# Put-off work spread over 32 groups instead of 8, and sum and difference in one VectorE operation

## The chip, the cores and the metric

The kernel runs on one core of a Trainium2 chip. The metric is the device time of one execution in microseconds. Before the change three executions took 2817.58, 2814.88 and 2814.3 us, a median of 2814.88 us.

The engines are named as in the profile: PE is TensorE's matmul, PEld its weight load, DVE is VectorE, ACT is ScalarE, POOL is GpSimd, SP is SyncE, which here only issues DMAs.

## What is computed

A Fourier transform along two axes, a gated two-matrix network with two matrices behind it, and a greedy routing of 24576 tokens to 8 experts of 3072 places each:

```python
def _attn_ref(x):                       # x: 8 x 3072 x 256
    X = np.fft.fft(x, axis=1)
    X = np.fft.fft(X, axis=2)
    return X.real.astype(np.float32)

def _moe_ref(x, w1, w2, w3, w_out):     # 256 -> 1024 -> 1024 -> 256
    a = x @ w1
    b = x @ w2
    h = a * b @ w3
    return (h @ w_out).astype(np.float32)

def _moe2_ref(x, w_gate, w1, w2):
    logits = x @ w_gate
    order = np.argsort(-logits.flatten())
    # greedy: best (token, expert) pairs first, each expert takes N // E tokens
    ...
    for e in range(E):
        mask = assigned == e
        h = np.maximum(x[mask] @ w1[e], 0.0)
        out[mask] = h @ w2[e]
```

## The kernel before

**Two stages.** Stage A makes the rows (transform, first network) and their logits, stage B routes them and runs the experts. All products run in split form: a value is a high part and a low part of type fp32r, and `mm3` makes three matmuls of one product (high by high, high by low, low by high).

**Stage A** works in 384 steps: 8 batches `b`, 2 sets `st`, 3 blocks `q`, 8 slices `f` of the hidden width. The 8 steps of one (b, st, q) are a group; there are 48 groups, and a group makes 512 rows. In one step, `front` makes the odd part `us` (6 matmuls of 256 columns) and the even part `ue` (one of 512 columns, six of 256) in two PSUM tiles `l1` of four. ACT copies `us` to `qs` (four buffers), DVE makes `ue + qs` and `ue - qs` into `pm` (one buffer) and multiplies its two halves into `ab`, which is `qs` again. One step later `parts` splits `ab`: ACT writes the high part `ah`, POOL the low part `al` (three buffers each). Three steps later `back` multiplies `ah` and `al` by the combined matrix `W` (`l2`: 12 matmuls of 264 columns, 256 of the row and 8 of the logits) into four PSUM tiles `acc`, one for each 128 of the 512 rows. At the group's end ACT moves them out and `store` writes rows (`xs_d`) and logits (`L`).

**Put off.** The last 8 groups (`ASIDE`) do not run `l2`. Their `ah` and `al` go to DRAM (`away`, two DMAs of 256 KB in a step on SP's queue), those of the very last group (`KEPT`) straight into the places of the two transform tables. Only their logits are made: `logits` runs two matmuls of 512 columns with the gate columns of `W` as weights (16 and 8 columns of weights), and at a group's end ACT copies the 16 x 512 result, PE turns it in four small products into an `acc` tile, and DVE writes it to `L`. In stage B `putoff` runs the 768 missing matmuls of 256 columns (L1371) while the first routing works.

**Beside the steps.** `dft_set` makes the next set's transform in four parts spread over the steps of `DFT_AT`. `fold_batch` makes the next batch's inputs, nearly all on POOL: 1.3 units of work are handed out in a step (`FOLD`), which spreads one batch's folding over some 26 steps, from the end of a batch's first group to the start of its fifth. `middle` (L921) is a small product for eight single rows in the last set.

**What sets the order.** PE, DVE, ACT and POOL run in the order in which the code is written (`manual_schedule`); the DMAs on SP are placed by the scheduler. In every step the order is `front`, `back` of three steps before, the multiplication, `parts` of the step before, then the things put off by `later`.

In stage A no matmul of type fp32r moves fewer than 256 columns; the second table is read 256 wide although a part of it has 192 or 193 columns:

```python
        w = 193 if kind % 2 else 192
        return tabs["B"][p0:p1, hl, base + t * w: base + t * w + 256]
```

Of the kernel before, what the change touches and what calls it, by code (L numbers as in the profile page):

```python
# [9 lines left out]
F32 = mybir.dt.float32  # L10
# [12 lines left out]
NT = N // 128  # L23
# [2 lines left out]
NF = FF // 128  # L26
FMAX = 3.4028234663852886e38
XW = 260
ASIDE, KEPT = 8, 1
SHARE = 864  # L30


# [192 lines left out]
@with_exitstack  # L225
def body(ctx, tc, I, out, nb=NB, dbg=None):
    nc = tc.nc
    vec, act, pool = nc.vector, nc.scalar, nc.gpsimd
    dram = ctx.enter_context(tc.tile_pool(name="dram", bufs=1, space=bass.MemoryType.DRAM))
    xs_d = dram.tile([N, XW], F32, name="xs_d")  # L230
    ed = dram.tile([2, NB, 3, 768], F32R, name="ed")
    em = dram.tile([3, NB], F32R, name="em")
    sp_d = dram.tile([8, NB, 128], F32R, name="sp_d")
    md = dram.tile([NB, D], F32, name="md")
    away = dram.tile([max(ASIDE - KEPT, 1), NF, 128, 2, 512], F32R, name="away")
# [24 lines left out]
    stage_b(tc, I, out, k)  # L260
# [19 lines left out]
def stage_a(ctx, tc, I, nb, k):  # L280
# [532 lines left out]
    def front(g):  # L813
# [10 lines left out]
                extras(steps[i])  # L824
        e3 = e3t[0]
        n = number(g)
        spill = 0 <= n < k.aside - KEPT

        qs = work.tile([128, 512], F32, name="qs", bufs=4)
        ab = qs.rearrange("p (s c) -> p s c", s=2)  # L830

        us, ue = l1(), l1()
        for w in range(2):
# [15 lines left out]
        if n >= 0:  # L849
            k.putoff[n, f] = None if spill else (ah, al)  # L850

        def parts():
            act.activation(ah, qs, AF.Copy)  # L853
            (vec if n == k.aside - 1 and f in LAST else pool).tensor_tensor(al, qs, ah, op=ALU.subtract)  # L854
# [18 lines left out]
        at = f % 4 * 1024  # L873
        return places[key][:, at:at + 512], places[key][:, at + 512:at + 1024]

    def logits(n, f, ahl, j0):

        if f == 0:
            acct[0] = accs(n % 4)
        a = acct[0]  # L880
# [4 lines left out]
        lt = work.tile([2 * E, 512], F32, name="xo")  # L885
        u = accs((n + 2) % 4)[:, :4 * E].rearrange("p (i e) -> p i e", i=4)
# [5 lines left out]
        later(1, lambda: act.activation(lt, a[:2 * E], AF.Copy))  # L892
        later(2, turn)
        later(3, lambda: vec.tensor_copy(L[:, :, j0:j0 + 4].rearrange("p e j -> p j e"), u))

    def back(g, ahl):
        b, st, q, f = g
        n = number(g)
        if n >= 0:
            logits(n, f, ahl, (b * 6 + st * 3 + q) * 4)  # L900
            return
        if f == 0:
            acct[0] = [accs(i) for i in range(4)]
        acc = acct[0]
        l2(acc, ahl[0], ahl[1], f, 4)
        if f < NF - 1:
            return
        j0 = (b * 6 + st * 3 + q) * 4
        for h in range(2):
            xo = work.tile([128, 2, 264], F32, name="xo")  # L910
            act.activation(xo[:, 0], acc[2 * h][:, :264], AF.Copy)
            (vec.tensor_copy(xo[:, 1], acc[2 * h + 1][:, :264]) if EV else act.activation(xo[:, 1], acc[2 * h + 1][:, :264], AF.Copy))
            later(1, lambda xo=xo, j=j0 + 2 * h: store(xo, j))

    def store(xo, j):
        pool.tensor_copy(L[:, :, j:j + 2].rearrange("p e j -> p j e"), xo[:, :, D:])
        pool.tensor_copy(xo[:, :, D:D + 4], sc["tok"][:, j:j + 2, None].to_broadcast([128, 2, 4]))
        nc.sync.dma_start(k.xs_d[j * 128:(j + 2) * 128].rearrange("(i p) d -> p i d", p=128), xo[:, :, :XW])


    def middle():  # L921
# [22 lines left out]
        xo = work.tile([128, 264], F32, name="qs", bufs=4)  # L944
        act.activation(xo[:NB], acc[:NB, :264], AF.Copy)
        nc.sync.dma_start(k.md, xo[:NB, :D])
        for b in range(nb):
            p, j = DUP[b]
            if b == nb - 1:
                yield  # L950
            nc.sync.dma_start(L[p:p + 1, :, j], xo[b:b + 1, D:])
            if j // 4 < nb * 6 - k.aside:
                nc.sync.dma_start(k.xs_d[j * 128 + p:j * 128 + p + 1, :D], xo[b:b + 1, :D])
        yield

# [62 lines left out]
def stage_b(ctx, tc, I, out, k):  # L1018
# [315 lines left out]
    def putoff():  # L1334
# [311 lines left out]
```

## Time and profile before

| what | us |
|---|---|
| median of three executions | 2814.88 |
| the profiled execution | 2810.5 |
| its span, first to last instruction | 2808.7 |
| stage A, steps of the first 40 groups | 111.0 to 1202.5 |
| steps of the last 8 groups (put off) | 1202.5 to 1384.5 |
| end of stage A, until the logits are complete | 1384.5 to 1394.7 |
| put-off products in stage B | 1394.7 to 1496.4 |
| rest of the first routing | 1496.4 to 1540 |
| experts | 1540 to 2808.7 |

The profiled execution took 4.4 us less than the median of the others. Busy shares over the whole span are PE 95%, PEld 87%, DVE 76%, ACT 47%, POOL 54%; a share is an average over stages with different limits. A matmul's recorded time is longer than its distance to the next one, because they overlap; what PE can do is read from the distances between starts.

### The profile page before, as it was taken

What the parts mean: (1) busy time and instruction counts of PE and PEld (TensorE: products, weight loads), DVE (VectorE), ACT (ScalarE), POOL (GpSimd) and SP (SyncE); (2) the same over time, 40 slices, a digit from 0 to 9 for tenths busy, and PEclk for the clock granted to TensorE, in tenths of its full rate; (3) what the DMA queues carried; (4) which work ended last, traced back from release to release, by engine and by line L of the source; (5) the groups of instructions that cost most, each with busy time, mean ns of one, the idle gap of its engine ahead of it and who ended that gap; (6) DMA issues with size and microseconds to landing.
All of it is one profiled execution on the core that took longest, in us unless ns stands there. A gap on an engine that the chain in (4) does not pass through costs nothing.

```text
span 2808.7 us, 51817 instructions
## 1 busy us (share of the span) xinstructions
PE 2674.4 (95%) x19903; PEld 2454.0 (87%) x19903; DVE 2135.4 (76%) x3795; ACT 1323.0 (47%) x2383; POOL 1518.0 (54%) x1529
## 2 busy tenths in 40 slices
PE   4999999999999999999996999989999999999998
PEld 2899999999999999987796788878888888889997
DVE  8788787978878797888877888788787878862222
ACT  2344444444444444444363747466573746543332
POOL 7295775939577593964304244353535435363532
PEclk8999999999999999999997999999999999999999
DMA  6410110101011011145394112211212122121211
GB/s 232 133 54 32 39 46 24 54 32 54 32 39 47 24 52 34 52 162 200 128 338 154 36 65 54 69 50 46 76 43 73 48 67 54 43 68 43 76 46 35
DMA packets 104705, 207.32 MB, mean 74 GB/s; under 512 B 35178, under 2 KB 60442, under 8 KB 99338
## 3 DMA queue, kind: packets, MB, share of 16 engines
q1 hardware_dynamic: 81000, 131.02, 13.7%
q0 software_dynamic: 22224, 72.58, 8.0%
q8 instruction: 157, 2.57, 0.4%
q14 instruction: 90, 0.74, 0.1%
q10 hardware_dynamic: 1234, 0.41, 0.1%
HBM read 118.15 MB, written 80.28 MB: 71 GB/s over the span
## 4 chain that ended last, share of the span: by engine, by line
PE 73%; DVE 17%; ACT 3%; issue 2%; DMA 1%; POOL 1%; another core or an unknown queue 0%; DVEq 0%; ACTq 0%; POOLq 0%; SPq 0%
PE yp L1483 13%; PE l L220 7%; PE l L222 7%; PE l L221 7%; PE acc L804 5%; PE acc L800 5%; PE acc L801 5%; PE hp L220 4%; PE hp L221 4%; PE hp L222 4%; DVE oR L1086 4%; PE l L836 3%; DVE W L1466 2%; ACT ja L1081 2%; PE hp L1371 2%
## 5 line engine op out<-in xcount | busy, mean ns | idle before, releaser
L854 POOL TENSOR_TENSOR al<-qs,ah 128x512 fp32r<-128x512 f32 x376 | 513.4, 1365 | 406.2 <-ACT ah L853 311.4
L1483 PE MATMUL yp<-FA,W 128*128 128x256 f32 x3040 | 622.0, 286 | 17.8 <-DVE W L1466 8.4
L1483 PEld LDWEIGHTS yp<-FA,W 128*128 128x128 f32 x3040 | 497.8, 190 | 44.6 <-ACT yo L1489 14.9
L859 DVE TENSOR_TENSOR qs<-pm 128x512 f32<-128x512 f32 x384 | 427.4, 1113 | 41.2 <-DVE pm L843 1.8
L853 ACT ACTIVATE ah<-qs 128x512 fp32r<-128x512 f32 x376 | 237.2, 631 | 358.2 <-DVE qs L859 317.7
L1466 DVE SCALAR_TENSOR_TENSOR W<-hp,W 128x512 fp32r<-128x512 f32 x336 | 230.1, 687 | 227.0 <-ACT W L1462 205.0
L1483 PE MATMUL yp<-FB,W 128*128 128x256 f32 x1520 | 388.0, 282 | 0.0
L842 DVE TENSOR_TENSOR pm<-l,qs 128x512 f32<-128x512 f32 x384 | 264.7, 689 | 149.4 <-PE l L222 116.2
L840 ACT ACTIVATE qs<-l 128x512 f32<-128x512 f32 x384 | 227.0, 591 | 235.3 <-PE l L222 220.0
L220 PE MATMUL hp<-tabA,tabB 128*128 128x512 f32 x768 | 319.5, 416 | 0.9 <-ACT tabA L1432 0.9
L1493 POOL DMA_INDIRECT out_dram<-yo,oi x188 | 191.7, 1020 | 231.3 <-DMA out_dram<-yo,oi 217.8
L1462 ACT ACTIVATE W<-hp 128x512 fp32r<-128x512 f32 x336 | 197.2, 593 | 251.6 <-PE hp L222 232.7
L221 PE MATMUL hp<-tabA,tabB 128*128 128x512 f32 x768 | 304.0, 396 | 6.0 <-DVE tabA L1436 6.0
L1483 PEld LDWEIGHTS yp<-FB,W 128*128 128x128 f32 x1520 | 287.9, 189 | 14.3
L800 PE MATMUL acc<-W,ah 128*128 128x264 f32 x1120 | 283.6, 284 | 0.0
L801 PE MATMUL acc<-W,ah 128*128 128x264 f32 x1120 | 283.3, 284 | 0.0
L1086 DVE TENSOR_SCALAR_CACHE_REDUCE oR<-oR,nx 128x1536 uint16<-128x1536 uint16 x196 | 281.4, 1459 | 0.0
L843 DVE TENSOR_TENSOR pm<-l,qs 128x512 f32<-128x512 f32 x384 | 261.2, 680 | 0.0
L1407 POOL DMA_INDIRECT xt<-xs_d,idx x192 | 194.9, 1015 | 109.1 <-issue 49.9
L1457 POOL TENSOR_TENSOR W<-xo,W 128x512 fp32r<-128x512 f32 x48 | 66.6, 1387 | 336.8 <-ACT W L1455 321.1
L222 PE MATMUL hp<-tabA,tabB 128*128 128x512 f32 x624 | 246.7, 395 | 0.0
L220 PE MATMUL l<-eo,SW 128*128 128x256 f32 x768 | 220.7, 287 | 0.0
(350 smaller groups left out, 6930.4 us busy)
## 6 DMA issues: line engine op xcount, KB each, us to landing
xs_d<-xo SPq DMA_DIRECT2D x96, 260.0 KB
xt<-in_xg_dram SPq DMA_DIRECT2D x24, 1024.0 KB
away<-ah SPq DMA_DIRECT2D x56, 256.0 KB
away<-al SPq DMA_DIRECT2D x56, 256.0 KB
yo<-away SPq DMA_DIRECT2D x28, 512.0 KB
raw<-in_w3t_dram SPq DMA_DIRECT2D x16, 512.0 KB
FA<-away SPq DMA_DIRECT2D x14, 512.0 KB
FB<-away SPq DMA_DIRECT2D x14, 512.0 KB
```

What stands on the lines that cost most here:

```text
L220: nc.tensor.matmul(out, ah, bh, start=start, stop=False, skip_group_check=True)
L221: nc.tensor.matmul(out, ah, bl, start=False, stop=False, skip_group_check=True)
L222: nc.tensor.matmul(out, al, bh, start=False, stop=stop, skip_group_check=True)
L800: nc.tensor.matmul(acc[i][:, :264], ah[:, a], W[0][:, f], start=f == 0, stop=False, skip_group_check=True)
L801: nc.tensor.matmul(acc[i][:, :264], ah[:, a], W[1][:, f], start=False, stop=False, skip_group_check=True)
L842: vec.tensor_tensor(pm[:, 0].rearrange("p w c -> p (w c)"), ue, qs, op=ALU.add)
L843: vec.tensor_tensor(pm[:, 1].rearrange("p w c -> p (w c)"), ue, qs, op=ALU.subtract)
L854: (vec if n == k.aside - 1 and f in LAST else pool).tensor_tensor(al, qs, ah, op=ALU.subtract)
L859: return ah, al, parts, lambda: vec.tensor_tensor(ab, pm[:, :, 0], pm[:, :, 1], op=ALU.mult)
L1086: vec.tensor_scalar(jk[:, :n], T[:, :n], nx[:, i:i + 1], None, op0=ALU.is_ge, op1=ALU.add, accum_out=acc[:, i:i + 1])
L1466: vec.scalar_tensor_tensor(hl, hp, 0.0, hh, op0=ALU.max, op1=ALU.subtract)
L1483: nc.tensor.matmul(yp[i], hhl[seq[s][0]][:, t[i]], seq[s][1], start=f == 0 and s == 0 and (i % 2 == 0 or len(yp) == 4), stop=f == NF - 1 a ...
```

## The change

There are now `4 * PUT` = 32 groups of the 48 that put something off, the last 32, and each puts off one quarter of its rows: the last 128 of 512. `back` runs `l2` for three `acc` tiles (9 matmuls of 264 columns) and, for the fourth, the two logits matmuls, now 128 columns wide. The logits' copy, turn and write at a group's end become one each, the turn now in an `l1` tile and the write to `L` on ACT. All groups use `ah` and `al` of `work`; in 32 groups two DMAs of 64 KB in a step take the last quarter to `away` (28 groups) or into the tables' places (4 groups).

In all 384 steps ACT makes two copies of the odd part, one with its sign turned, into `pm` itself (three buffers; `qs` is gone), and DVE adds the even part to both in one operation of 1024 elements. The product stands in `pm`, from which ACT and POOL read it.

```diff
-ASIDE, KEPT = 8, 1
+PUT, KEPT = 8, 1
+ASIDE = 4 * PUT
...
     def front(g):
-        spill = 0 <= n < k.aside - KEPT
-        qs = work.tile([128, 512], F32, name="qs", bufs=4)
-        ab = qs.rearrange("p (s c) -> p s c", s=2)
+        m, side = n // 4, slice(n % 4 * 128, n % 4 * 128 + 128)
+        pm = work.tile([128, 2, 2, 256], F32, name="pm", bufs=3)
+        two = pm.rearrange("p s w c -> p s (w c)")
+        ab = pm[:, :, 0]
...
-        act.activation(qs, us, AF.Copy)
-        pm = work.tile([128, 2, 2, 256], F32, name="pm", bufs=1)
-        vec.tensor_tensor(pm[:, 0].rearrange("p w c -> p (w c)"), ue, qs, op=ALU.add)
-        vec.tensor_tensor(pm[:, 1].rearrange("p w c -> p (w c)"), ue, qs, op=ALU.subtract)
-        if n < 0 or spill:
-            ah = work.tile([128, 512], F32R, name="ah", bufs=3)
-            al = work.tile([128, 512], F32R, name="al", bufs=3)
-        else:
-            ah, al = put(f)
+        act.activation(two[:, 0], us, AF.Copy)
+        act.activation(two[:, 1], us, AF.Copy, scale=-1.0)
+        vec.tensor_tensor(two, ue[:, None, :].to_broadcast([128, 2, 512]), two, op=ALU.add)
+        ah = work.tile([128, 512], F32R, name="ah", bufs=3)
+        al = work.tile([128, 512], F32R, name="al", bufs=3)
...
         def parts():
-            act.activation(ah, qs, AF.Copy)
...
+            act.activation(ah2, ab, AF.Copy)
...
-            if spill:
-                cp(nc.sync, k.away[n, f, :, 0], ah)
-                cp(nc.sync, k.away[n, f, :, 1], al)
+            if n >= 0:
+                cp(nc.sync, away[0], ah[:, 384:])
+                cp(nc.sync, away[1], al[:, 384:])
...
-        nc.tensor.matmul(a[:2 * E], gates[0][:, f], ahl[0], start=f == 0, stop=False, skip_group_check=True)
-        nc.tensor.matmul(a[:E], gates[0][:, f, :E], ahl[1], start=False, stop=f == NF - 1, skip_group_check=True)
+        nc.tensor.matmul(a[:2 * E, :128], gates[0][:, f], ahl[0][:, 384:], start=f == 0, stop=False, skip_group_check=True)
+        nc.tensor.matmul(a[:E, :128], gates[0][:, f, :E], ahl[1][:, 384:], start=False, stop=f == NF - 1, skip_group_check=True)
...
         def turn():
-            for i in range(4):
-                nc.tensor.matmul(u[:, i], lt[:, i * 128:(i + 1) * 128], sc["twice"][:2 * E], start=i == 0, stop=i == 3, skip_group_check=True)
+            u.append(l1()[:, :E])
+            nc.tensor.matmul(u[0], lt, sc["twice"][:2 * E], start=True, stop=True, skip_group_check=True)
...
-        later(3, lambda: vec.tensor_copy(L[:, :, j0:j0 + 4].rearrange("p e j -> p j e"), u))
+        later(3, lambda: act.activation(L[:, :, j], u[0], AF.Copy))
...
     def back(g, ahl):
-        n = number(g)
-        if n >= 0:
-            logits(n, f, ahl, (b * 6 + st * 3 + q) * 4)
-            return
+        n = 3 if number(g) >= 0 else 4
...
-        l2(acc, ahl[0], ahl[1], f, 4)
+        l2(acc, ahl[0], ahl[1], f, n)
+        xos = [work.tile([128, 2, 264], F32, name="xo") for h in range(2)] if f == NF - 1 else [None] * 2
+        if n < 4:
+            logits(acc[3], f, ahl, j0 + 3, xos[1][:2 * E, 1, :128] if f == NF - 1 else None)
```

The order on PE, one step of batch 3, set 0, block 2 (in the changed kernel the groups from batch 2, set 1, block 1 on put off). `l` is a PSUM tile of `front`, `acc` one of `back`; before:

```order
L800 MATMUL acc_7894<-W_437,ah 128x264
L801 MATMUL acc_7894<-W_438,ah 128x264
L804 MATMUL acc_7891<-W_437,al 128x264
L804 MATMUL acc_7892<-W_437,al 128x264
L804 MATMUL acc_7893<-W_437,al 128x264
L804 MATMUL acc_7894<-W_437,al 128x264
L220 MATMUL l_7920<-eo_6569,SW_79 128x256
```

And of the changed kernel, the same step; `xo` holds the finished logits of the group before:

```order
L801 MATMUL acc_7777<-W_437,ah 128x264
L802 MATMUL acc_7777<-W_438,ah 128x264
L805 MATMUL acc_7775<-W_437,al 128x264
L805 MATMUL acc_7776<-W_437,al 128x264
L805 MATMUL acc_7777<-W_437,al 128x264
L878 MATMUL acc_7778<-ah,gates 16x128
L879 MATMUL acc_7778<-al,gates 8x128
L886 MATMUL l_7801<-small,xo 128x8
L221 MATMUL l_7807<-eo_6445,SW_79 128x256
```

The three matmuls of the fourth `acc` tile are gone, two of 128 columns stand in their place in every step, and a turn once in a group.

The order on ACT at the same place, before:

```order
L840 ACTIVATE qs<-l_7870 128x512
L853 ACTIVATE ah<-qs 128x512
L378 ACTIVATE FB_7369<-FO 128x4x128
L840 ACTIVATE qs<-l_7920 128x512
L853 ACTIVATE ah<-qs 128x512
L840 ACTIVATE qs<-l_7959 128x512
```

And after:

```order
L842 ACTIVATE pm<-l_7755 128x512
L843 ACTIVATE pm<-l_7755 128x512
L853 ACTIVATE ah<-pm 128x512
L379 ACTIVATE FB_7251<-FO 128x4x128
L842 ACTIVATE pm<-l_7807 128x512
L843 ACTIVATE pm<-l_7807 128x512
L853 ACTIVATE ah<-pm 128x512
L890 ACTIVATE L<-l_7801 128x8
```

A second copy stands ahead of every `ah`, and once in a group the write to `L`.

The order on DVE there, before:

```order
L842 TENSOR_TENSOR pm<-l_7871,qs 128x512
L843 TENSOR_TENSOR pm<-l_7871,qs 128x512
L859 TENSOR_TENSOR qs<-pm 128x512
L379 TENSOR_TENSOR FB_7370<-FO,FB_7369 128x4x128
L842 TENSOR_TENSOR pm<-l_7921,qs 128x512
```

And after:

```order
L844 TENSOR_TENSOR pm<-l_7756,pm 128x1024
L859 TENSOR_TENSOR pm<-pm 128x2x256
L380 TENSOR_TENSOR FB_7252<-FO,FB_7251 128x4x128
L844 TENSOR_TENSOR pm<-l_7808,pm 128x1024
L859 TENSOR_TENSOR pm<-pm 128x2x256
```

Two operations became one of twice the length; the multiplication stays.

## Rows read from the trace of the kernel before

**Rows 1.** Windows: length, busy us (count) PE PEld DVE ACT POOL, clock, DMA share, GB/s.

```profile
111.00:1202.50 1091.50, 1090.84 (x8550) 1064.03 (x8549) 895.26 (x1159) 474.89 (x899) 766.85 (x751) 1.00 0.13 44
1202.50:1384.50 182.00, 173.84 (x1175) 145.12 (x1173) 158.61 (x225) 84.57 (x155) 87.86 (x74) 1.00 0.48 177
1384.50:1394.70 10.20, 5.38 (x17) 2.36 (x15) 6.39 (x16) 4.28 (x6) 2.66 (x3) 0.63 0.00 0
1394.70:1496.40 101.70, 100.22 (x810) 98.42 (x810) 78.82 (x197) 51.37 (x83) 6.07 (x18) 0.97 0.93 335
```

**Rows 2.** The same: a plain group, six groups' sum, a put-off group.

```profile
495.80:520.70 24.90, 24.90 (x202) 24.55 (x201) 23.40 (x26) 11.43 (x22) 24.49 (x25) 1.00 0.20 65
...
sum 164.00, PE 163.95 PEld 160.21 DVE 134.28 ACT 71.50 POOL 113.64; mean PE 27.32 PEld 26.70 DVE 22.38 ACT 11.92 POOL 18.94
...
1297.40:1318.40 21.00, 19.25 (x129) 16.00 (x129) 19.23 (x26) 9.50 (x17) 10.27 (x9) 1.00 0.54 202
```

**Rows 3.** Order of time in a step: start us, length us, engine, line; `[idle <-releaser]`.

```profile
540.01 0.28 PE L220 MATMUL l<-eo,CW 128*128 128x256 f32 x1
...
540.07 1.74 POOL L854 TENSOR_TENSOR al<-qs,ah 128x512 fp32r<-128x512 f32 x1
540.12 0.28 PE L221 MATMUL l<-eo,CW 128*128 128x256 f32 x1
...
540.71 0.29 PE L800 MATMUL acc<-W,ah 128*128 128x264 f32 x1
...
540.83 0.29 PE L801 MATMUL acc<-W,ah 128*128 128x264 f32 x1
...
541.87 0.54 PEld L804 LDWEIGHTS acc<-W,al 128*128 128x128 f32 x4 [0.24 <-POOL al L854]
```

**Rows 4.** Order of time around two logits matmuls in a put-off group, PE and PEld.

```profile
1382.27 0.39 PE L882 MATMUL acc<-tabA,gates 128*8 128x512 f32 x1
1382.50 0.28 PE L220 MATMUL l<-eo,SW 128*128 128x256 f32 x1
...
1382.04 0.09 PEld L882 LDWEIGHTS acc<-tabA,gates 128*8 128x8 f32 x1
1382.27 0.19 PEld L220 LDWEIGHTS l<-eo,SW 128*128 128x128 f32 x1
```

**Rows 5.** One group's turn, first and last start; four transposes on the chain.

```profile
L890 PE MATMUL acc<-small,xo x8: 251/251/272, 1237.7 to 1238.5; 16*128 16x8 f32 x8
...
1542.28 0.44 PE tp L1428 x4
```

**Rows 6.** Groups of instructions: count, busy us, mean ns, idle before and releasers.

```profile
L842 DVE TENSOR_TENSOR pm<-l,qs 128x512 f32<-128x512 f32 x384 | 264.7, 689 | 149.4 <-PE l L222 116.2 <-ACT qs L840 9.1 <-PE acc L804 0.5
L843 DVE TENSOR_TENSOR pm<-l,qs 128x512 f32<-128x512 f32 x384 | 261.2, 680 | 0.0
L859 DVE TENSOR_TENSOR qs<-pm 128x512 f32<-128x512 f32 x384 | 427.4, 1113 | 41.2 <-DVE pm L843 1.8 <-POOL al L854 0.5
L379 DVE TENSOR_TENSOR eo<-sF,eo 128x768 fp32r<-128x768 f32 x32 | 30.7, 959 | 25.9 <-ACT eo L378 25.9
L840 ACT ACTIVATE qs<-l 128x512 f32<-128x512 f32 x384 | 227.0, 591 | 235.3 <-PE l L222 220.0 <-POOL al L854 10.5 <-POOL L L916 3.4
```

**Rows 7.** Two windows of one folding, all engines; then `front`'s 512-column matmul alone.

```profile
474.20:487.00 12.80, 12.80 (x102) 12.35 (x101) 8.29 (x13) 5.69 (x12) 8.63 (x12) 1.00 0.12 42
487.00:554.30 67.30, 67.25 (x537) 65.90 (x537) 63.07 (x71) 29.83 (x56) 66.61 (x64) 1.00 0.15 49
...
487.00:554.30 67.30, 8.27 (x21) 1.00 0.15 49
```

**Rows 8.** Order of time at the end of stage A.

```profile
1384.03 0.28 PE L222 MATMUL l<-eo,CW 128*128 128x256 f32 x1
...
1390.48 0.69 DVE L854 TENSOR_TENSOR tabB<-qs,tabB 128x512 fp32r<-128x512 f32 x1 [0.50 <-ACT tabB L853]
...
1394.41 0.21 DVE L894 COPY L<-acc 128x32 f32<-128x32 f32 x1 [3.23 <-PE acc L890]
...
1394.67 8.47 PEld L1371 LDWEIGHTS hp<-W,tabA 128*128 128x128 f32 x48 [0.40 <-DVE L L894]
```

More of the change, by code (lines that the diff above doesn't have):

```diff
@@ L234, in body @@
     md = dram.tile([NB, D], F32, name="md")
-    away = dram.tile([max(ASIDE - KEPT, 1), NF, 128, 2, 512], F32R, name="away")
+    away = dram.tile([max(PUT - KEPT, 1), NF, 128, 2, 512], F32R, name="away")
     keep = ctx.enter_context(tc.tile_pool(name="keep", bufs=1))
@@ L839, in front @@
             mm3(nc, o, CW[0][:, w, fs(f)], CW[1][:, w, fs(f)], Eh[:, c], El[:, c], False, True)
-        act.activation(qs, us, AF.Copy)
-        pm = work.tile([128, 2, 2, 256], F32, name="pm", bufs=1)
-        vec.tensor_tensor(pm[:, 0].rearrange("p w c -> p (w c)"), ue, qs, op=ALU.add)
-        vec.tensor_tensor(pm[:, 1].rearrange("p w c -> p (w c)"), ue, qs, op=ALU.subtract)
-        if n < 0 or spill:
-            ah = work.tile([128, 512], F32R, name="ah", bufs=3)
-            al = work.tile([128, 512], F32R, name="al", bufs=3)
-        else:
-            ah, al = put(f)
+        act.activation(two[:, 0], us, AF.Copy)
[3 more added lines that the diff above has]
+        al = work.tile([128, 512], F32R, name="al", bufs=3)
         if n >= 0:
-            k.putoff[n, f] = None if spill else (ah, al)
+            k.putoff[m, f] = None if m < PUT - KEPT else put(f)
+            away = [k.away[m, f, :, h, side] for h in range(2)] if m < PUT - KEPT else [t[:, side] for t in put(f)]
         def parts():
-            act.activation(ah, qs, AF.Copy)
-            (vec if n == k.aside - 1 and f in LAST else pool).tensor_tensor(al, qs, ah, op=ALU.subtract)
-            if spill:
-                cp(nc.sync, k.away[n, f, :, 0], ah)
-                cp(nc.sync, k.away[n, f, :, 1], al)
+            ah2, al2 = (t.rearrange("p (s c) -> p s c", s=2) for t in (ah, al))
+            act.activation(ah2, ab, AF.Copy)
+            (vec if n == k.aside - 1 and f in LAST else pool).tensor_tensor(al2, ab, ah2, op=ALU.subtract)
+            if n >= 0:
+                cp(nc.sync, away[0], ah[:, 384:])
+                cp(nc.sync, away[1], al[:, 384:])
         return ah, al, parts, lambda: vec.tensor_tensor(ab, pm[:, :, 0], pm[:, :, 1], op=ALU.mult)
@@ L904, in back @@
         acc = acct[0]
-        l2(acc, ahl[0], ahl[1], f, 4)
+        l2(acc, ahl[0], ahl[1], f, n)
+        xos = [work.tile([128, 2, 264], F32, name="xo") for h in range(2)] if f == NF - 1 else [None] * 2
+        if n < 4:
+            logits(acc[3], f, ahl, j0 + 3, xos[1][:2 * E, 1, :128] if f == NF - 1 else None)
         if f < NF - 1:
             return
[L908 to L913, printed above, removed]
+        for h, xo in enumerate(xos):
+            for i in range(min(n - 2 * h, 2)):
+                act.activation(xo[:, i], acc[2 * h + i][:, :264], AF.Copy)
+            later(1, lambda xo=xo[:, :min(n - 2 * h, 2)], j=j0 + 2 * h: store(xo, j))
     def store(xo, j):
-        pool.tensor_copy(L[:, :, j:j + 2].rearrange("p e j -> p j e"), xo[:, :, D:])
-        pool.tensor_copy(xo[:, :, D:D + 4], sc["tok"][:, j:j + 2, None].to_broadcast([128, 2, 4]))
-        nc.sync.dma_start(k.xs_d[j * 128:(j + 2) * 128].rearrange("(i p) d -> p i d", p=128), xo[:, :, :XW])
+        n = xo.shape[1]
+        pool.tensor_copy(L[:, :, j:j + n].rearrange("p e j -> p j e"), xo[:, :, D:])
+        pool.tensor_copy(xo[:, :, D:D + 4], sc["tok"][:, j:j + n, None].to_broadcast([128, n, 4]))
+        nc.sync.dma_start(k.xs_d[j * 128:(j + n) * 128].rearrange("(i p) d -> p i d", p=128), xo[:, :, :XW])
     def middle():
@@ L943, in middle @@
         yield
-        xo = work.tile([128, 264], F32, name="qs", bufs=4)
+        xo = fold.tile([128, 8, 128], F32, name="FO").rearrange("p a b -> p (a b)")[:, :264]
         act.activation(xo[:NB], acc[:NB, :264], AF.Copy)
@@ L1348, in finish @@
         def finish(n, acc):
-            j0 = NT - 4 * ASIDE + 4 * n
+            g0 = NT // 4 - ASIDE + 4 * n
+            rows = xrows.rearrange("(g a p) d -> p g a d", a=4, p=128)
             for i in range(2):
@@ L1352, in finish @@
                 act.activation(xo[:, :, :D], acc[i], AF.Copy)
-                j = j0 + 2 * i
-                pool.tensor_copy(xo[:, :, D:], k.sc["tok"][:, j:j + 2, None].to_broadcast([128, 2, 4]))
-                nc.sync.dma_start(xrows[j * 128:(j + 2) * 128].rearrange("(i p) d -> p i d", p=128), xo)
+                g = g0 + 2 * i
+                pool.tensor_copy(xo[:, :, D:], k.sc["tok"][:, 4 * g + 3:4 * g + 8:4, None].to_broadcast([128, 2, 4]))
+                nc.sync.dma_start(rows[:, g:g + 2, 3], xo)
             for b, (p, j) in enumerate(DUP):
-                if j0 <= j < j0 + 4:
+                if g0 <= j // 4 < g0 + 4 and j % 4 == 3:
                     nc.sync.dma_start(xrows[j * 128 + p:j * 128 + p + 1, :D], k.md[b:b + 1])
```

13 lines of the change are left out of this document (5 added, 8 removed).

## The prediction

> **What bounds the kernel now.** I read the windows by stage first, then those of single groups, the order of time inside a step, the groups of instructions, and the end of stage A. [rows 1] In the first 40 groups PE is busy for 1090.84 of 1091.50 us, so they are PE's. [rows 2] A group without transforms takes 24.9 us, 3.11 us a step. [rows 3, 4] Inside a step a matmul of 256 or 264 columns starts 0.12 us before the next, one of 512 columns 0.23 us: 12 x 0.12 + 0.23 for `front` and 12 x 0.12 for `back` are 3.11 us, all of the step. POOL stands close behind: in the same group it is busy for 24.49 of 24.90 us, because the folding lies there.
>
> In the last eight groups it is otherwise. A put-off step costs PE 1.67 + 2 x 0.23 = 2.13 us, but [rows 2] a group takes 21.0 us, 2.62 us a step: a chain of DVE, ACT and POOL sets it. PE's work in [rows 1] the 182.0 us is 64 x 2.13 = 136.3; transforms 14.6 (six groups take 164.0 against 6 x 24.9, and the last eight groups hold as many parts); the small product `middle` some 7.5 (16 matmuls of 0.23, 24 of 0.12, 8 of 0.115); seven turns of eight short matmuls 6.4 [rows 5]; and three `back` steps still with 12 matmuls, 2.9 more. That is 167.7, so PE stands idle for 14.3 us. [rows 8] Then 10.3 us pass from the last `front` to complete logits, nearly idle, and only then PE begins the put-off products, which [rows 1] fill it again (100.22 of 101.70). The change moves work from a PE-bound stretch into these holes; it takes none away.
>
> **PE's step in the 32 groups.** Three matmuls of 264 columns go: -0.36 us. Two logits matmuls of 128 columns come, and the trace has none of this type and width. The first streams half of 256 columns: by the 0.11 us between 256 and 512 columns, 0.06. Behind the second, weights of 128 columns must be loaded, whose load is recorded at 0.19 us against 0.09 for 8 columns [rows 4]; [rows 5] eight matmuls of only 8 columns behind such weights start 0.8 / 7 = 0.115 apart. So 0.17 for the pair, with 0.12 (two times 0.06) and 0.22 (the transposes of 128 columns of plain fp32 in rows 5, 0.11 each) as its near ends; I take 0.17, because the weight load is the same instruction. The far end, 0.23 each, is a rival below. A step becomes 1.67 + 1.08 + 0.17 = 2.92 us, 0.19 less than 3.11.
>
> The Trainium skill (TensorE: Matmul & The Clock Gate, Back-to-back issue gap) gives 81 ns as sustained distance of matmuls of 128 columns with their weight loads; by it the pair would be an estimated 0.16 us and the sum 2 to 3 us lower. No run here shows it yet.
>
> **Groups 16 to 39.** 192 steps x 0.19 = 36.5 us gained. One turn in each of 24 groups is new: two short matmuls with exposed weight loads, 0.23 us, 5.5 together. Net -31.0, if PE stays the bound.
>
> **POOL in the foldings.** It doesn't quite. [rows 7] Over 21 steps of a folding POOL is busy for 66.61 of 67.30 us, 3.2 us a step, and PE 67.25; [rows 3] at 541.87 PE has already waited 0.24 us for POOL's `al`, so the reserve that PE had ahead of the stretch is used up there. With 0.19 less a step PE would want 63.3 us and gets 67.3 less what POOL can begin earlier: ahead of the stretch POOL idles 12.80 - 8.63 = 4.2 us, of which I give it half. That is 2 us lost in each of the four foldings inside the 32 groups: +8. Ends: 0, and 26 steps x 0.19 x 4 = 20.
>
> **The last eight groups** become PE-bound: 64 x 2.92 + 14.6 + 7.5 + 8 x 0.23 = 210.8 us, three `back` steps behind the last `front` counted in. Behind PE's last product come the end of the chain, copies and a turn, and it waits once for it: from the last `front` some 0.3 + 1.24 + 1.1 + 0.63 + 0.69 on ACT and DVE, 1.1 for the last products, 1.5 for copies and turn, near 7 us, 3.2 more than the three `back` steps. Logits are complete at 1202.5 + 210.8 + 3.2 = 1416.5 against 1394.6: +21.9 us here.
>
> **The clock.** [rows 1] At the end of stage A, after PE stood idle, its granted clock is 0.63 on average, a mix of the two levels, and [rows 8] the first 48 put-off products take 8.47 us, 0.18 each instead of 0.12. With fuller PE I give back 2 of these 3 us.
>
> **VectorE, ScalarE, DMAs.** [rows 6] DVE's pair takes 0.69 + 0.68; one operation of 1024 elements 1.24, by 0.96 for 768 and 0.68 for 512 (ends 1.18 and 1.37). That is 0.13 us a step, 50 us of DVE time, of which the path gets nothing: PE's 2.92 us cover DVE's 2.62. Without that cover it would be worth up to 0.13 us a step. ACT's second copy is 0.59 us, 4.7 in a group, where [rows 2] ACT is busy for 11.43 of 24.90; it reaches DVE some 0.3 us later, inside the three steps of lag. Its new wait is for POOL's `al` of three steps before instead of four (`pm` has three buffers, `qs` had four); behind it on ACT stands `ah` of the step before and so POOL's next `al`, but in the foldings DVE reaches that step later still. The turn takes an `l1` tile once a group, so one `us` waits for DVE instead of ACT. SP issues 512 DMAs of 64 KB in place of 112 of 256 KB; ahead of rows, small loads and 1 MB inputs on its queue. The same bytes spread over four times as many steps, and [rows 1] the eight groups bore them at a DMA share of 0.48. I cost these at nothing.
>
> **The sum.** -31.0 + 8 + 21.9 - 2 = -3.1 us. Against the profiled execution's 2810.5 that is 2807.4; the median of the others is 4.4 above it, so 2814.88 - 3.1, rounded to 2812. What this kernel's measurement can tell from no change is about 0.2%, 5.6 us: the forecast is no visible change. With 4 to 12 for the foldings and the pair within 0.02, its own range is 2804 to 2820.
>
> **Rivals.**
> First, faster: POOL recovers all its idle time and the foldings cost nothing (-8), and the short pair costs 0.14 because the next weights load partly under it (-7.7). 2797. For it: POOL's 4.2 us of idle time ahead of the stretch nearly cover the 4.9 that 26 steps save. Against it: rows 3's wait.
>
> Second, slower: POOL sets the pace of the whole folding. Nothing is gained over 26 steps (20 instead of 8), and each folding's end leaves PE behind POOL by what three buffers instead of four allow, some 1 us: 2827. It decides if POOL's idle time ahead of the stretch stays. For it: 66.61 of 67.30 us.
>
> Third, much slower: a matmul of 128 columns is paced as one of 512, 0.23 us. Then a step takes 3.21, more than before; 256 x 0.29 = 74 us more, and the foldings' 8 fall away: 2878. For it: nothing of this type under 256 columns is streamed in stage A, and a table is read 256 wide where 193 would do. Against it: no row shows such a step, and plain fp32 needs 0.11 for 128 columns.
>
> Fourth, the change doesn't hide its DMAs: 1 MB inputs ahead of a 64 KB DMA hold `ah` longer than three steps, an estimated 3 us for four loads or so: 2825.
>
> **How the numbers follow.** Forecast 0.47 (of this faster 0.10, same 0.33, slower 0.04), first rival 0.20 (all faster), second 0.18 (slower 0.15, same 0.03), third 0.10, fourth 0.05 (both slower). Faster 0.30, same 0.36, slower 0.34. A range from 2796 to 2832 holds the forecast and most of the first two rivals and the fourth, and leaves out the third.
>
> **What would show it.** Right: plain groups from 16 on near 23.4 us with PE full; distances of 0.06 and 0.115 at the two logits matmuls; folding groups above 24; the last eight groups without idle PE; complete logits at about 1391 us; one VectorE operation near 1.24 us. Wrong: 0.2 us behind each logits matmul; PE waiting for `al` throughout the foldings; ACT waiting on POOL or DMAs in every step; put-off products beginning late although the logits are complete.

## The result, and the profile after

The changed kernel takes 2835.33 us (median of five, 2829.79 to 2841.6) against 2814.88: a ratio of 1.0076, with a 95% interval of 1.006 to 1.0091. It is 20.5 us slower, and the time lies above the predicted range of 2796 to 2832.

The profiled executions span 2808.7 us before and 2830.1 after. I cut both at the first 512-column matmul of `front` in groups 16 and 40, and at the first and last put-off product, all read from the order of time:

| stretch (us) | before | forecast | after | difference |
|---|---|---|---|---|
| to group 16 | 546.3 | 546.3 | 545.8 | -0.5 |
| groups 16 to 39 | 656.2 | 633.2 | 639.6 | -16.6 |
| groups 40 to 47, to complete logits | 192.2 | 214.1 | 218.3 | +26.1 |
| put-off products | 101.0 | 99 | 110.2 | +9.2 |
| rest (routing's end, experts) | 1313.0 | 1313.0 | 1316.2 | +3.2 |

Against the forecast of -3.1, 24.5 us are missing: 6.4 in groups 16 to 39, 4.2 in the last eight, 11.2 in the put-off products, 3.2 in the rest, less the 0.5 at the start.

The windows by stage after the change, in the columns of [rows 1]:

```profile
111.00:1185.40 1074.40, 1065.52 (x8403) 1029.16 (x8402) 852.94 (x839) 616.94 (x1242) 769.47 (x750) 1.00 0.21 65
1185.40:1374.90 189.50, 189.05 (x1494) 178.34 (x1493) 143.86 (x142) 108.00 (x221) 86.16 (x92) 1.00 0.22 66
1374.90:1403.70 28.80, 27.81 (x225) 26.38 (x223) 21.41 (x26) 17.56 (x36) 12.00 (x17) 1.00 0.23 68
1403.70:1514.00 110.30, 99.54 (x810) 96.36 (x810) 79.74 (x200) 50.96 (x81) 4.79 (x17) 1.00 0.91 312
```

Beside [rows 1] three things changed. PE now has gaps in the first 40 groups: 1065.52 of 1074.40 us, where it had been 1090.84 of 1091.50. The last eight groups are full, and the granted clock is 1.00 (2.4 GHz) to the end of stage A, where it had been 0.63 in the last 10 us. And the put-off products, which had filled PE for 100.22 of 101.70 us, now leave 10.8 us open, at a DMA share of 0.91.

Next a group without transforms (group 44) and two groups that hold a folding (20 and 21), after the change, in the same columns:

```profile
1295.40:1319.20 23.80, 23.80 (x197) 23.12 (x195) 18.97 (x18) 14.30 (x29) 12.44 (x13) 1.00 0.21 63
655.10:705.50 50.40, 48.55 (x391) 46.51 (x390) 39.15 (x36) 29.71 (x62) 50.00 (x48) 1.00 0.32 100
```

The same two folding groups before the change:

```profile
659.90:710.40 50.50, 50.45 (x403) 49.31 (x402) 46.88 (x53) 22.89 (x45) 49.89 (x48) 1.00 0.20 64
```

The plain group fell from 24.9 us [rows 2] to 23.8. The two folding groups fell by 0.1 in 50: POOL is busy for 50 us in both, and most of what PE's lighter work saved became idle time, 1.85 us of it.

The pair of logits matmuls and a turn stand in the order of time after the change (start us, length us, engine, line):

```profile
1394.49 0.52 PE L805 MATMUL acc<-W,al 128*128 128x264 f32 x3
1394.85 0.22 PE L878 MATMUL acc<-ah,gates 128*16 128x128 f32 x1
1394.91 0.22 PE L879 MATMUL acc<-al,gates 128*8 128x128 f32 x1
1394.96 0.33 PE L221 MATMUL l<-eo,SW 128*128 128x256 f32 x1
1395.14 0.27 PE L222 MATMUL l<-eo,SW 128*128 128x256 f32 x1
...
1306.24 0.22 PE L879 MATMUL acc<-al,gates 128*8 128x128 f32 x1
1306.39 0.38 PE L886 MATMUL l<-small,xo 16*128 16x8 f32 x2
1306.70 0.39 PE L221 MATMUL l<-eo,SW 128*128 128x256 f32 x1
1306.93 0.29 PE L222 MATMUL l<-eo,SW 128*128 128x256 f32 x1
```

The pair's two matmuls start 0.06 us before what follows them, and the matmul of `front` behind them is followed after 0.18 instead of 0.12: the load of 128 columns of weights shows there, one instruction later than I had placed it. Over the pairs without a turn behind them the three parts are 0.058, 0.060 and 0.055 in the middle, together 0.173. With a turn, 0.46 pass from L879 to L221 instead of 0.06, and 0.23 instead of 0.18 behind it: a turn costs 0.46 us.

VectorE, ScalarE and POOL in stage A (groups of instructions: count, busy us, mean ns, idle before and releaser):

```profile
L854 POOL TENSOR_TENSOR al<-pm,ah 128x512 fp32r<-128x512 f32 x383 | 530.1, 1384 | 413.7 <-ACT ah L853 312.9
L844 DVE TENSOR_TENSOR pm<-l,pm 128x1024 f32<-128x1024 f32 x384 | 469.3, 1222 | 228.3 <-ACT pm L843 196.3
L859 DVE TENSOR_TENSOR pm<-pm 128x512 f32<-128x512 f32 x384 | 422.4, 1100 | 13.2
L842 ACT ACTIVATE pm<-l 128x512 f32<-128x512 f32 x384 | 228.8, 596 | 381.6 <-PE l L223 226.7
```

The one VectorE operation takes 1.222 us in place of 0.689 and 0.680 [rows 6].

Where the put-off products lose their time is seen on SP, which issues their loads in order. SP after the change, in one of six such places:

```profile
1484.47 0.97 SPq L1352 DMA_DIRECT2D xs_d<-xo  x2
1485.57 0.39 SPq L217 DMA_DIRECT2D yo<-away  x1
1487.51 0.33 SPq L217 DMA_DIRECT2D FA<-away  x1
1495.38 0.48 SPq L1355 DMA_DIRECT2D xs_d<-md  x1
1495.95 0.53 SPq L217 DMA_DIRECT2D yo<-away  x1
1496.58 0.38 SPq L217 DMA_DIRECT2D FA<-away  x1
```

And what PE's weight loads waited for between 1403.7 and 1514 us (engine, tile and line, releaser: us in total, times, longest):

```profile
PEld yp L1368 <- DMA yo<-away: 5.8, 6, 1.9
PEld yp L1368 <- DMA FB<-away: 2.0, 1, 2.0
PEld hp L1368 <- DMA yo<-away: 1.9, 1, 1.9
...
PEld hp L1368 <- DMA FA<-away: 0.9, 1, 0.9
PEld yp L1368 <- DMA FA<-away: 0.8, 1, 0.8
```

L1355 copies a single row of 1 KB (the rows made by `middle`, one of each batch) into `xs_d`, over a row that the store at L1352 has just written. SP issues it only when that store of 260 KB has landed. From the load ahead of it SP issues nothing for 7.9 us, and six loads of put-off data stand behind it. The change puts off tiles of six batches instead of two, so there are six such copies instead of two, five of them among the loads instead of one; the four others there took 3.9, 9.0, 7.2 and 7.2 us. PE then waits 11.4 us for put-off data, where the same wait had been 0.2 us.

The Trainium skill (DMA: Bandwidth & Descriptors, Anatomy of one DMA — SWDGE (gpsimd) path), in a section on DMAs that GpSimd issues, says that the DMA engines do not wait on semaphores: such a wait is made by the issuing sequencer before dispatch. The rows of SP agree: SP is silent for 7.9 us while it holds a copy of 1 KB.

### The profile page after: what moved, and what is told of

Its sections match the earlier page's. It is cut to its first block, busy times and chain, and to the rows that moved or that the text cites. A ratio compares the mean times of both kernels' runs of the same rounds, so it can differ in the third digit from the quotient of the medians.

```text
span 2830.1 us, 53229 instructions
## 1 busy us (share of the span) xinstructions
PE 2685.8 (95%) x20287; PEld 2477.0 (88%) x20287; DVE 2093.5 (74%) x3403; ACT 1502.1 (53%) x2823; POOL 1523.7 (54%) x1561
## 3 DMA queue, kind: packets, MB, share of 16 engines
q8 instruction: 160, 2.62, 0.4%
## 4 chain that ended last, share of the span: by engine, by line
PE 70%; DVE 13%; POOL 6%; DMA 3%; ACT 3%; issue 3%; another core or an unknown queue 0%; SPq 0%; POOLq 0%; ACTq 0%; DVEq 0%
PE yp L1480 13%; PE l L221 8%; PE l L223 7%; PE l L222 7%; PE hp L221 4%; PE hp L222 4%; PE acc L805 4%; PE hp L223 4%; PE acc L801 4%; PE acc L802 4%; DVE oR L1082 3%; PE l L838 3%; POOL al L854 2%; DVE W L1463 2%; ACT ja L1077 2%
## 5 line engine op out<-in xcount | busy, mean ns | idle before, releaser
L854 POOL TENSOR_TENSOR al<-pm,ah 128x512 fp32r<-128x512 f32 x383 | 530.1, 1384 | 413.7 <-ACT ah L853 312.9
L844 DVE TENSOR_TENSOR pm<-l,pm 128x1024 f32<-128x1024 f32 x384 | 469.3, 1222 | 228.3 <-ACT pm L843 196.3
L859 DVE TENSOR_TENSOR pm<-pm 128x512 f32<-128x512 f32 x384 | 422.4, 1100 | 13.2
L842 ACT ACTIVATE pm<-l 128x512 f32<-128x512 f32 x384 | 228.8, 596 | 381.6 <-PE l L223 226.7
L221 PE MATMUL hp<-tabA,tabB 128*128 128x512 f32 x768 | 320.7, 418 | 0.9 <-ACT tabA L1429 0.9
L853 ACT ACTIVATE ah<-pm 128x512 fp32r<-128x512 f32 x384 | 243.5, 634 | 70.4 <-DVE pm L859 26.1
L1404 POOL DMA_INDIRECT xt<-xs_d,idx x192 | 194.9, 1015 | 118.3 <-DVE A L1286 51.3
L221 PE MATMUL l<-eo,SW 128*128 128x256 f32 x768 | 232.7, 303 | 0.0
L1077 ACT ACTIVATE ja<-oR,nx 128x1536 bf16<-128x1536 uint16 x98 | 154.5, 1577 | 139.2 <-DVE cur L1112 112.0
```

The lines of the kernel that those rows point to most:

```text
L221: nc.tensor.matmul(out, ah, bh, start=start, stop=False, skip_group_check=True)
L844: vec.tensor_tensor(two, ue[:, None, :].to_broadcast([128, 2, 512]), two, op=ALU.add)
L853: act.activation(ah2, ab, AF.Copy)
```

## The experiments

Each run is timed against the kernel before on the same chip. Stretches are those of the table. Each comes from one profiled execution, and the chips differ: even the stretch to group 16, in runs where nothing there is edited, goes from 545.8 to 546.6 us, and the rest (routing's end and experts) differs by up to 18 us over all runs and is not used.

**Single-row copies later.** The copies of one put-off group are issued at the finish of the next:

```
 def finish(n, acc):
+    patch()          # the copies kept from the group before
     ...
     if g0 <= j // 4 < g0 + 4 and j % 4 == 3:
-        nc.sync.dma_start(xrows[...], k.md[b:b + 1])
+        patches.append((b, p, j))
```

> The changed kernel, with each single-row copy into xs_d (L1355) issued one put-off group later, behind the fetches instead of ahead of them. Queue theory: each such copy waits on SP for the 260 KB store ahead of it to land (4.9, 9.0, 7.2, 7.2 and 7.9 us in the trace of the changed kernel) and the fetches of put-off data stand behind it; then the 111 us from the first put-off product to the last copy become 101 to 104, PE waits for fetched data for 0 to 3 us instead of 21, and the time is 2824 to 2828. Rival, the rate of the DMAs: their share is 0.82 to 1.04 in that stretch anyway, so waits only move; the stretch stays at 108 or more and the time at 2832 or more.

Measured: 2821.32 us, ratio 1.0032 (1.002 to 1.0044). The window of the put-off products in this run, columns as above:

```profile
1404.30:1502.30 98.00, 96.98 (x810) 95.63 (x810) 78.30 (x194) 51.01 (x81) 4.64 (x16) 1.00 0.98 350
```

and one copy in it on SP:

```profile
1477.05 0.32 SPq L217 DMA_DIRECT2D FB<-away  x1
1477.42 0.47 SPq L1348 DMA_DIRECT2D xs_d<-md  x1
1479.35 1.07 SPq L1360 DMA_DIRECT2D xs_d<-xo  x2
1480.51 0.52 SPq L217 DMA_DIRECT2D yo<-away  x1
```

The products take 97.9 us from first to last start instead of 110.2, at a DMA share of 0.98 instead of 0.91, and PE waits for no put-off data any more. The copy goes 0.4 us behind the load ahead of it. The queue theory holds, and the gain was larger than expected. Against the kernel before, the stretch is now 3.1 us shorter. Most of that is the clock term of the prediction (2 us): [rows 1] have 0.97 over 101.7 us of this stretch, this run 1.00, and the weight loads of the first 48 products, which took 8.47 us before [rows 8], take 5.8 in this run and in the changed kernel, whose row is

```profile
1403.70 5.75 PEld L1368 LDWEIGHTS hp<-W,tabA 128*128 128x128 f32 x48 [0.36 <-ACT L L890]
```

It isn't so in every run: in the next one, whose stage A ends in the same way, they take 7.28 us, at a granted clock of 0.97 over the stretch.

**Folding thinner.**

```
-LAG, FOLD, EV, AH, W8 = 3, 1.3, 0, 1, 1
-FOLD_AT = 3
+LAG, FOLD, EV, AH, W8 = 3, 1.17, 0, 1, 1
+FOLD_AT = 0
```

> The changed kernel, with the folding begun three steps earlier and spread thinner (1.17 units a step instead of 1.3, 29 steps instead of 26). Pace theory: PE's 4.1 us of new idle time in each folding come from POOL's 3.2 us a step; at about 3.0 a step more than half of that goes, so idle time of groups 16 to 39 falls from 36 to 24 to 29 us and the time to 2823 to 2830. Rival, the third buffer: ACT waits for one of three pm buffers to come free whatever POOL's pace; idle time stays above 33 us and the time within 3 us of 2835.

Measured: 2825.84 us, ratio 1.0051 (1.0037 to 1.0064), within the time expected. Groups 16 to 39 take 635.3 us instead of 639.6. PE's idle time there, counted from distances of matmul starts over the usual ones, fell from 36.2 to 31.7 us, less than the pace theory had said. (This count holds also what shows of weight loads, 10.6 us behind the pairs alone, and some 14 us in the kernel before.) The same two folding groups:

```profile
650.60:700.30 49.70, 48.70 (x395) 46.85 (x395) 40.98 (x36) 29.88 (x62) 49.46 (x47) 1.00 0.32 100
```

POOL is still busy for 49.46 of 49.70 us. That fits pace as the cause, with 29 steps too few to take POOL off the path; the next run looks at the rival.

**Spread without the VectorE part.** `front` and `parts` are those of before (one copy into `qs`, four buffers; two VectorE operations); all else is the changed kernel.

> The changed kernel without its VectorE part: one copy into qs (four buffers) and two VectorE operations, as before the change; the spread over 32 groups stays. Rival, the third buffer: with four buffers ACT no longer waits for POOL in the foldings, the idle time of groups 16 to 39 falls by 10 us or more and the time to 2825 or less. Pace theory: POOL sets the pace with four buffers too; idle time within 4 us, time 2831 to 2839.

Measured: 2830.41 us, ratio 1.0065 (1.0053 to 1.0078). This tells apart what looked alike in the trace. Waits between 600 and 1200 us, changed kernel:

```profile
ACT pm L842 <- POOL al L854: 85.6, 59, 2.9
...
PEld acc L805 <- POOL al L854: 11.7, 16, 1.0
```

The first row is large: ScalarE waits for POOL to free one of three `pm` buffers. With four buffers it is 2.1 us, yet groups 16 to 39 take 640.4 us instead of 639.6. The wait is only the place where POOL's pace becomes visible. (This run takes back the VectorE operation too, so it shows the two together.)

**VectorE part alone.** The kernel before, with `pm` in three buffers, two copies by ScalarE and one operation:

```
-act.activation(qs, us, AF.Copy)
-vec.tensor_tensor(pm[:, 0]..., ue, qs, op=ALU.add)
-vec.tensor_tensor(pm[:, 1]..., ue, qs, op=ALU.subtract)
+act.activation(two[:, 0], us, AF.Copy)
+act.activation(two[:, 1], us, AF.Copy, scale=-1.0)
+vec.tensor_tensor(two, ue[:, None, :].to_broadcast([128, 2, 512]), two, op=ALU.add)
```

> The kernel before with the VectorE part alone: two signed copies by ScalarE, one operation of 1024 elements, three pm buffers; the last eight groups are put off as before. If VectorE's time is covered in the first 40 groups, nothing is gained there; in the last eight, where a chain of VectorE, ScalarE and POOL sets the pace, 0.13 us in 64 steps would give up to 8 us back: 2807 to 2815. If the third buffer counts, ScalarE waits for POOL in all seven foldings, some 1 us each or more: 2815 to 2825.

Measured: 2815.98 us, ratio 1.0013 (1.0004 to 1.0021). The time is that of the third buffer, its cause is not: the first 40 groups, in which the foldings lie, grew by 1.4 us only. There was no gain in the last eight groups, which a chain through VectorE sets: 194.9 us instead of 192.2. VectorE between 1275 and 1320 us of this run (groups of instructions):

```profile
L860 DVE TENSOR_TENSOR pm<-pm 128x512 f32<-128x512 f32 x16 | 21.6, 1347 | 0.6
L843 DVE TENSOR_TENSOR pm<-l,pm 128x1024 f32<-128x1024 f32 x16 | 19.4, 1215 | 0.7 <-PE l L222 0.5
```

The same stretch of the kernel before:

```profile
L859 DVE TENSOR_TENSOR qs<-pm 128x512 f32<-128x512 f32 x17 | 17.9, 1053 | 1.8
L842 DVE TENSOR_TENSOR pm<-l,qs 128x512 f32<-128x512 f32 x17 | 11.8, 692 | 1.9
L843 DVE TENSOR_TENSOR pm<-l,qs 128x512 f32<-128x512 f32 x16 | 10.9, 681 | 0.0
```

The single operation saves 0.16 us, and the multiplication behind it became 0.29 us longer. Why shows in the order of time of the changed kernel, where VectorE's multiplication (L859) meets POOL's `al` (L854):

```profile
1298.12 1.52 DVE L859 TENSOR_TENSOR pm<-pm 128x512 f32<-128x512 f32 x1
...
1304.32 0.69 DVE L859 TENSOR_TENSOR pm<-pm 128x512 f32<-128x512 f32 x1
...
1297.81 1.29 POOL L854 TENSOR_TENSOR al<-pm,ah 128x512 fp32r<-128x512 f32 x1 [1.40 <-PE acc L879]
...
1304.52 1.63 POOL L854 TENSOR_TENSOR al<-pm,ah 128x512 fp32r<-128x512 f32 x1 [2.73 <-ACT ah L853]
```

A multiplication that starts while `al` runs ends 0.54 us after it and takes 1.52 us; one that starts first takes 0.69, and then `al` takes 1.63 instead of 1.29. In both stretches above every multiplication starts while `al` runs, so starting it earlier only makes it longer. The order of time of this run shows what sets the pace there:

```profile
1296.92 1.21 DVE L843 TENSOR_TENSOR pm<-l,pm 128x1024 f32<-128x1024 f32 x1
1297.69 1.29 POOL L855 TENSOR_TENSOR al<-pm,ah 128x512 fp32r<-128x512 f32 x1 [1.34 <-ACT ah L854]
1298.16 1.37 DVE L860 TENSOR_TENSOR pm<-pm 128x512 f32<-128x512 f32 x1
1299.61 0.63 ACT L854 ACTIVATE ah<-pm 128x512 fp32r<-128x512 f32 x1 [1.03 <-issue]
1300.32 1.28 POOL L855 TENSOR_TENSOR al<-pm,ah 128x512 fp32r<-128x512 f32 x1 [1.34 <-ACT ah L854]
```

From one `al` to the next pass 1.29 us, 0.55 to the multiplication's end, 0.63 for `ah` and two gaps of 0.08: 2.63 us, the step of a put-off group. The sum and difference are not in this chain; here they end 0.85 us before `al` does. What made the eight groups 2.7 us longer is not settled.

The Trainium skill (SBUF — State Buffer, SBUF: two separate sides) calls this an exclusive lock: a VectorE operation with two inputs in SBUF and a GpSimd operation that reads SBUF take a shared pair of ports in turn, each for its whole length. The rows agree: the multiplication ends 0.54 us after `al`.

**Both single edits together.**

> The changed kernel with both single edits together: single-row copies one group later, and the folding begun three steps earlier at 1.17 units a step. If the two causes are separate, their gains add: put-off products begin near 1398.4 us, take 98 us, and the time is 2811 to 2815, that of the kernel before. If they share a cause (put-off work waits for something else once the copies are gone), 2817 or more.

Measured: 2806.57 us against 2803.24 for the kernel before, ratio 1.001 (1.0001 to 1.0019), some 3 us slower. Put-off products begin at 1397.3 us and take 97.8: the two causes add.

**The same edits on the kernel before,** as a control:

> The kernel before with the same two edits (late single-row copies, folding begun earlier and thinner), as a control. PE waited neither for put-off data (0.2 us) nor long for POOL in the foldings, so both should give little: 2808 to 2814. If they give 9 us or more, they are general gains and say nothing on what the change cost.

Measured: ratio 0.9979 (0.997 to 0.9988), 5.5 us faster. Stage A ends 4.2 us earlier, the put-off products take 1.6 us less, of which the first 48 alone give 1.1. So the thinner folding is a gain of its own; only the copies belong mostly to the change. With both repaired, the change still costs 0.3% against the kernel before with the same repairs.

**Two tiles in 16 groups.** The pair gets 256 columns, two tiles of `l2` go; copies later as above:

```
-nc.tensor.matmul(a[:2 * E, :128], gates[0][:, f], ahl[0][:, 384:], ...)
+nc.tensor.matmul(a[:2 * E, :256], gates[0][:, f], ahl[0][:, 256:], ...)
```

> The changed kernel with late single-row copies, but two of four l2 tiles put off in the last 16 groups (32 to 47) instead of one in 32; logits matmuls have 256 columns. Theory of the pair: four pairs of 128 columns cost four times 0.175 us and four turns, where one pair of 512 costs 0.46; two pairs of 256 should cost 0.24 each, so PE's work falls. Step 2.63 us in plain groups, about 12 us gained in groups 32 to 39 (the foldings stay at POOL's pace), about 8 lost in the last eight; put-off products begin at 1388 to 1392 and the time is 2803 to 2808. Rival: the pair of 256 columns costs 0.3 or more, or the last eight groups fall back to the chain's 2.6 us and above with idle PE; then 2812 or more.

Measured: ratio 0.9996 (0.9987 to 1.0005), 10 us better than one tile in 32 groups with the same late copies (1.0032), but not the expected 0.997 or so: by its ratio this is the rival's time. Put-off products begin at 1396.3 instead of 1388 to 1392. The pair was right, as the order of time of the next run (the same two-tile step) shows:

```profile
1293.43 0.28 PE L880 MATMUL acc<-ah,gates 128*16 128x256 f32 x1
1293.54 0.28 PE L881 MATMUL acc<-al,gates 128*8 128x256 f32 x1
1293.66 0.27 PE L222 MATMUL l<-eo,SW 128*128 128x256 f32 x1
1293.78 0.28 PE L223 MATMUL l<-eo,SW 128*128 128x256 f32 x1
```

Two times 0.12, and no exposed load behind them. Nor did the last eight groups fall back to the chain: PE is busy for 200.14 of their 203.5 us. What failed is the foldings again: in groups 33, 38 and 39 PE idles 4.5, 4.0 and 4.9 us.

**The same, in groups without a folding.** Put off in groups 23 to 25, 29 to 31, 35 to 37 and 41 to 47:

> As the 16 groups with two tiles put off, but in groups 23 to 25, 29 to 31, 35 to 37 and 41 to 47, those in which POOL does not fold. If the loss in groups 16 to 39 comes from POOL's pace in the foldings alone, nine groups gain 3.5 us each without a loss behind them, the last eight groups take about 10 us more than before the change, put-off products begin at 1372 to 1378 and the time is 2788 to 2796. Rival: the reserve that POOL builds ahead of a folding is used up by the lighter groups, so the folding takes back what they gained; then 2803 or more.

Measured: ratio 0.9985 (0.9976 to 0.9994); put-off products begin at 1390.4. By its ratio the time is the rival's, but its reason is only part of it. Groups 23, 24 and 25 gain 2.4, 3.1 and 2.7 us instead of 3.5 each, and group 26, in which the next folding runs, gives 1.5 back: the lighter groups ahead of it use up POOL's reserve. The last eight cost 14.7 instead of 10.

**Placed, with thinner folding.**

> Sixteen groups with two tiles put off (23 to 25, 29 to 31, 35 to 37, 41 to 47), late single-row copies, and the folding begun earlier at 1.17 units a step. If the 2.3 us of idle time in group 26 and its like are POOL's pace in the folding that follows the lighter groups, about half goes: put-off products begin at 1383 to 1387 instead of 1390.4, ratio to the kernel before 0.996 to 0.9975. Rival: the lighter groups use up POOL's reserve whatever the folding's pace; ratio 0.998 or more.

Measured: 2801.53 us, ratio 0.9958 (0.9944 to 0.9972). Put-off products begin at 1384.6, as expected from POOL's pace; group 26 idles 1.8 us instead of 2.7.

**Mixed.** Four tiles in groups 41, 42, 45 and 46, two in 24, 29, 30, 35, 36, 43, 44 and 47:

> Late single-row copies, thinner folding, and put-off work put where PE's work and the chain of the other engines balance: all four tiles in groups 41, 42, 45 and 46 (which hold transforms or the small product), two tiles in 24, 29, 30, 35, 36, 43, 44 and 47. Theory, PE's work and idle time add up by group: the last eight groups lose the 10 us of idle time that all-quarter or all-half groups there turn into PE work, five earlier groups gain some 3 us each; put-off products begin at 1378 to 1384, ratio 0.993 to 0.996. Rival: groups with all tiles put off stay bound by the chain of VectorE, ScalarE and POOL as before the change and give the gain back; ratio 0.9965 or more.

Measured: ratio 0.9976 (0.9967 to 0.9985): the rival. Groups with all tiles put off stay bound by the chain: PE idles 5.4 us in group 42 alone. In group 47, which puts off two, it idles 8.0 up to complete logits. Put-off products begin at 1386.9 us instead of 1378 to 1384.

**Mixed, two VectorE operations.**

> The same as the mixed kernel, with two VectorE operations on one copy (qs, four buffers) instead of one operation on two signed copies. Theory, from the run with the VectorE part alone (ratio 1.0013): one operation doesn't shorten the chain, because ScalarE's second copy and the later start of VectorE cost more than 0.13 us there; so this is 1 to 4 us faster than the mixed kernel, mostly in groups 41 to 47. Rival: VectorE's time sets the pace of the groups with all tiles put off; then it is 2 us or more slower.

Measured: ratio 0.9969 (0.9957 to 0.9982), 2 us better than the mixed kernel; the intervals overlap. In its trace group 42 idles 3.2 us instead of 5.4, and the last eight groups take 198.0 us instead of 203.5. The sign agrees with the run of the VectorE part alone; the size is not settled.

**Placed, two VectorE operations.**

> The placed halves with late single-row copies and thinner folding, ratio 0.9958, now with two VectorE operations on one copy instead of one on two signed copies. With two tiles put off PE is full in groups 41 to 46, so VectorE's part should count little there; what it can change is the end of stage A and the groups next to the foldings. Theory, the second copy by ScalarE costs and the single operation gives nothing: put-off products begin 0 to 4 us earlier than 1384.6, ratio 0.994 to 0.996. Rival: VectorE's 0.13 us a step counts; ratio 0.997 or more.

Measured: 2799.39 us against 2814.68, ratio 0.9949 (0.9936 to 0.9963), the fastest version: 15 us under the kernel before and, by the ratios, some 35 under the changed one. Put-off products begin at 1382.3 us. It has the late copies, the thinner folding, halves in the placed groups, and nothing of the VectorE part. Against the placed kernel with one operation (0.9958) the intervals overlap.

## Why the prediction was wrong

**PE's step: right.** Forecast 0.17 for the pair, measured 0.173. The third rival (0.23 for each matmul) is out. The 0.16 of the Trainium skill (TensorE: Matmul & The Clock Gate, Back-to-back issue gap) was near too, though the distances are not equal.

**The turn: mis-sized.** Forecast 0.23, measured 0.46: its two matmuls and the first one behind it start 0.15, 0.13 and 0.18 us after what stands ahead, where I had counted two loads of 0.115. (Counted in that way the seven turns before came to 6.4 us; by the order of time they add 7 x 1.18 = 8.3.) Over 24 groups the 0.23 too few are 5.5 us; the rest of the group came out a little better, so a plain group gained 1.17 us (24.94 to 23.77) instead of 1.29. Groups 16 to 39 would have gained 28.1 instead of 31.0 with PE full.

**The foldings: right mechanism, too small.** Groups 16 to 39 gained 16.6, so 11.5 us went, where I took 8 (ends 0 and 20, and 4 to 12 in the forecast's own range). This lies between the forecast and the second rival. Groups 20 and 21 gain nothing, as in the rival; but POOL's idle time ahead did not stay, as the rival needs: in group 19 it fell from 4.3 us to 1.8, and that group gained 1.0. The rival's buffer part is not seen: three or four buffers made no difference.

**The last eight groups: +26.1 instead of +21.9.** Every term was a little short: eight turns (1.8), the transforms and `middle` (some 1), the end of the chain (28.8 us from the last group's first step to complete logits, 5 more than a plain group, where I had added 3.2). The sign "complete logits at about 1391 us" does not follow from the prediction's own terms, which give 1202.5 - 23 + 210.8 + 3.2 = 1393.5; measured are 1403.7.

**The put-off products: the step that failed.** I let the clock give back 2 us and costed SP's queue at nothing. The clock gave back some 2.7, of the 3.1 that the run with late copies shows. But in the list of what the change moves I counted the spills and loads and not the single-row copies, which the diff shows as a changed condition at the end of `finish`. They are six DMAs of 1 KB, and they cost 12.3 us, half of the 24.5 that are missing; with late copies the time is 2821.32, inside the range, though still not the forecast of no visible change. The fourth rival had the right kind (a DMA that is not hidden, and its 2825) at the wrong place: 1 MB loads ahead of spills in stage A, where the trace after has a single wait of an engine for a DMA, of 1.7 us.

**VectorE, ScalarE: right.** 1.222 us for 1.24, and nothing gained on the path. But "without that cover it would be worth up to 0.13 us a step" is wrong. The 2.62 us that I called VectorE's are the step of a chain of `al`, the multiplication's end and `ah`, in which the sum and difference are not; where that chain sets the pace the run of the VectorE part alone gained nothing.

**The rest, +3.2 us,** is not settled: executions of one and the same kernel differ by more than that.

**What the sum hid.** The change was meant to fill PE's idle time in the last eight groups, and it did: counted from matmul starts, 25 us of idle time there became 10. But it pays PE for it. Logits and turns take 64 x 0.46 + 8 x 1.18 = 38.9 us before (a turn of 512 columns adds 1.18 to PE's order of time) and 256 x 0.173 + 32 x 0.46 = 59.0 after, 20.1 more for the same rows; in halves it is 128 x 0.235 + 16 x 0.73 = 41.8. This fits what was measured: halves with late copies are 10 us better than quarters with them, and the quarters stay 0.3% behind the kernel before even with both repairs.

## What to carry to other kernels

Count every DMA that a moved step issues, also the smallest: on a queue that issues in order, a 1 KB copy that must wait for a large store to land holds everything behind it until then, and issuing it later removes the cost. Work moved into another engine's idle time pays only if it doesn't grow on the way; cut it into pieces large enough that their fixed parts (an exposed weight load, a turn) stay hidden or few. Where two engines are within a few per cent of each other, lightening the first gains only the distance to the second: place the work in the stretches where the second has room.

## What the runs showed of the hardware

A matmul of 128 columns behind weights of 8 or 16 columns is paced at 0.06 us, and the exposed part of a 128-column load shows one instruction later, 0.055 us; behind a matmul of 256 columns nothing shows. Of two stores of 260 KB issued within 1 us, the one that a copy waited for had landed only 8 to 10 us later in four of five places (read from when the copy was issued), at a DMA share near 0.9. A VectorE multiplication with both inputs in SBUF took 0.69 us alone and 1.52 when POOL's subtraction had begun first. In the stretch of the VectorE part alone, all 16 of them ended 0.55 us after the subtraction, whether they took 0.88 us or 1.47. So an earlier operation on VectorE that is made shorter can be given back whole by the next.
